# Two products of the identity with itself ahead of the low products of later weight pieces

## The chip, the cores and the metric

The kernel runs on one core of a Trainium2 chip. The time is device microseconds of one execution; the median of three runs of the kernel before is given below, and one further execution was taken with the hardware profiler. The engines are TensorE (PE, with its weight loads as PEld), VectorE (DVE), ScalarE (ACT), GpSimd (POOL) and SyncE (SP, which issues all transfers here).

## What is computed

A gated linear attention over 768 steps (4 batches of 8 heads of 48), then two feed-forward layers on its output. Cut to what matters:

```python
for t in range(S):                                   # attention, state 48x48 per head
    state = alpha[t] * state + outer(k[t], v[t])
    y[t] = q[t] @ state
h = relu(x @ w_in)                                   # first layer, 384 -> 1024
conv = sum(conv_w[k] * shifted(h, k) for k in range(3))
x = (h * sigmoid(conv)) @ w_out                      # 1024 -> 384
xn = (x - mean(x)) / sqrt(var(x) + 1e-6) * g_ln      # second layer
out = x + relu(xn @ w_ch1) @ w_ch2                   # 384 -> 1536 -> 384
```

The weights arrive as 64-bit floats.

## The kernel before

The 24 attention chunks (128 steps each, chunk 0 to 23) are computed in a parallel form: two scans on DVE give the running products of alpha (`later`, `a`), POOL multiplies them into k and q, PE makes scores `s`, DVE masks them (`pm`), PE makes the output `y` and the state update `u`. Two chunks make a block of 256 rows; there are 12 blocks. A block goes through the first layer (`h`, 8 groups of 128 columns, then `acc`), the norm, a turn on PE (`h<-ident,xn`, halves 0 and 1, each split by ACT and DVE into `xnh` and `xnl`) and the second layer (`h<-xnh`, 12 groups, then `acc`).

Every product is made from a high and a low half of its operands. The four weights are called w1 (`w_in`), w2 (`w_out`), w3 and w4; each comes in pieces of two groups (4 pieces of w1 and w2, 6 of w3 and w4). `convert_weight` makes one piece: ACT writes a scaled copy `z` (L257) and the top bits (L261), DVE joins them in two instructions (L264, L267), ACT writes the high half (L306). The low half of w1, w2 and the first half of w4 is made by PE in `low_products`: identity times `z` (L310) less the high half (L311) into a PSUM bank, which ACT copies out (L314). This is done for group i = 0 and i = 1 of the piece. There are two `z` tiles and two PSUM banks of the tag `att`, used in turn; from chunk 3 on the attention uses these banks too.

The order of the instructions on every engine is set by `Plan`: each step has an engine, an estimated time, the tiles that it reads and writes, and a turn. `order` plays the steps with these estimates and writes each engine's list down; on the chip every engine then follows its list in order, and a step that waits holds up what stands behind it. So a step that is added, or one estimate, can move steps of every engine. Tiles that are handed out with `new` are handed out in the order in which the steps were added.

Of the kernel before, what the change touches and what calls it, by code (L numbers as in the profile page):

```python
# [21 lines left out]
DM = H * D  # L22
# [33 lines left out]
CONVERT_PACE = 1.25, 1, 1   # L56
BY_PE = 2, 0
LATER = 0, 8
LOW2 = "pool" 
LOWS = "pe", "pe", "pool", "pe"   # L60


class Plan:
# [11 lines left out]
    def ring(self, tag, n):  # L75

        self.sizes[tag] = n
        m = self.made[tag] = self.made.get(tag, -1) + 1
        return (tag, m)

    def add(self, engine, us, fn, r=(), w=(), new=(), port=False, mode=None, chain=None):

        if self.direct:
            fn()
            return
        me = len(self.steps)
        w = list(w) + list(new)
        needs = {self.wrote[b] for b in list(r) + w if b in self.wrote}
        for b in w:
            needs.update(self.read.get(b, ()))  # L90
        starts = set()
        for b in new:
            key = b[0], chain
            if key in self.first:
                starts.add(self.first[key])
            self.first[key] = me
        for b in r:
            self.read.setdefault(b, set()).add(me)
        for b in w:
            self.wrote[b], self.read[b] = me, set()  # L100
        needs.discard(me)
        starts.discard(me)
        mine = [b for b in set(list(r) + w) if b[0] in self.sizes]
        for b in mine:
            self.uses[b] = self.uses.get(b, 0) + 1
        new = [b for b in new if b[0] in self.sizes]
        self.steps.append((engine, us, fn, needs, starts - needs, port, mode, self.turn, mine, new))
# [93 lines left out]
def act_us(n, scaled=False):  # L201
    return 0.165 + 0.00083 * n + 0.093 * scaled


def dve_us(n, rate=1):
    return 0.15 + 0.00104 * rate * n


def pool_us(n):
    return 0.13 + 0.00215 * n  # L210
# [7 lines left out]
def attn_moe_kernel(ctx: ExitStack, tc, qka, vv, qka_t, v_t, w_in, conv_w, w_out, g_ln, w_ch1, w_ch2, out):  # L218
    nc = tc.nc
    pe, act, dve, pool, sp = nc.tensor, nc.scalar, nc.vector, nc.gpsimd, nc.sync  # L220
    plan = Plan()
    add, ring = plan.add, plan.ring
# [4 lines left out]
    ident = const.tile([128, 128], F32, name="ident")  # L227
# [6 lines left out]
    low = const.tile([R, NC], F32, name="low")  # L234
# [13 lines left out]
    def bank(tag, name):  # L248
        return psum.tile([128, 512], F32, tag=tag, name=name, bufs={"h": HB, "acc": NT + 1, "att": 2}[tag])

    def from_f64(z, raw, n):

        low, high = raw[:, :n, 0], raw[:, :n, 1]
        zi = z.bitcast(I32)

        def first():
            act.activation(out=z, in_=high.bitcast(F32), func=ACTF.Copy, scale=2.0 ** -112)  # L257

        def top():
            byte = raw[:, :n, :].bitcast(U8)[:, :, 3]  # L260
            act.activation(out=low, in_=byte, func=ACTF.Copy, scale=1 / 32, bias=-15.5 / 32)  # L261

        def join():
            dve.scalar_tensor_tensor(  # L264
                out=zi, in0=zi, scalar=3, in1=low, op0=ALU.logical_shift_left, op1=ALU.bitwise_or
            )
            dve.scalar_tensor_tensor(  # L267
                out=zi, in0=high, scalar=-(2 ** 31), in1=zi, op0=ALU.bitwise_and, op1=ALU.bitwise_or
            )

        yield first
        yield top
        yield join
# [3 lines left out]
    def weight_tile(n, j, dtype):  # L277
        return const.tile([128, PIECE, 2, DM], dtype, tag=f"w{n}_{j}", name=f"w{n}_{j}", bufs=1)
# [12 lines left out]
    def convert_weight(n, dst, j):  # L291
        m, w, z = PIECE * DM, (f"w{n}", j), ring("z", ZB)
        t = {}

        def first():
            t["z"] = wk.tile([128, m], F32, tag="z", name="z", bufs=ZB)
            raw = raw_w.pop((n, j)).rearrange("p j s f -> p (j s f)")
            t["f"] = list(from_f64(t["z"], raw.rearrange("p (n w) -> p n w", w=2), m))
            t["f"][0]()

        def high():
            t["w"] = weight_tile(n, j, F32R)
            for i in range(PIECE):
                dst[j * PIECE + i] = t["w"][:, i]
            t["z"] = t["z"].rearrange("p (j f) -> p j f", j=PIECE)
            act.activation(out=t["w"][:, :, 0], in_=t["z"], func=ACTF.Copy)  # L306

        def low_products(i):
            t[i] = bank("att", "low")[:, :DM]
            pe.matmul(out=t[i], lhsT=ident, rhs=t["z"][:, i], start=True, stop=False)  # L310
            pe.matmul(out=t[i], lhsT=minus, rhs=t["w"][:, i, 0], start=False, stop=True)  # L311

        def low_half(i):
            act.activation(out=t["w"][:, i, 1], in_=t[i], func=ACTF.Copy)  # L314

        def rest(engine):
            engine.tensor_tensor(out=t["w"][:, :, 1], in0=t["z"], in1=t["w"][:, :, 0], op=ALU.subtract)

        add("act", act_us(m), first, r=[w], new=[z])
        add("act", act_us(m), lambda: t["f"][1](), w=[w])  # L320
        add("dve", 2 * dve_us(m), lambda: t["f"][2](), r=[w], w=[z], port=True)
        add("act", act_us(m), high, r=[z], w=[w])
        low = LOW2 if n > 2 and j >= F2 // 2 // PIECE else LOWS[n - 1]
        if low == "pe":
            for i in range(PIECE):
                b = ring("att", 2)
                add("pe", 0.9, lambda i=i: low_products(i), r=[z, w], new=[b], mode="full")
                add("act", act_us(DM), lambda i=i: low_half(i), r=[b], w=[w])
        elif low == "dve":
            add("dve", dve_us(m), lambda: rest(dve), r=[z], w=[w], port=True)  # L330
        else:
            add("pool", pool_us(m), lambda: rest(pool), r=[z], w=[w], port=True)
# [9 lines left out]
    raw, vraw, prep, post, att = {}, {}, {}, {}, {}  # L342
# [584 lines left out]
            act.activation(out=hi[:, :, t:t + n], in_=src, func=ACTF.Copy)  # L927
            dve.tensor_tensor(out=lo[:, :, t:t + n], in0=src, in1=hi[:, :, t:t + n], op=ALU.subtract)

    def warm(n):  # L930

        ps = bank("h", "warm")
        for _ in range(n):
            pe.matmul(out=ps[:, :128], lhsT=ident, rhs=ident, start=True, stop=True)

    def load_small():
        t = {}

        def load():
            sp.dma_start(out=cwr.rearrange("p n w -> p (n w)"), in_=conv_w.bitcast(I32))  # L940
            sp.dma_start(out=gl, in_=g_ln.rearrange("(o f) -> o f", o=1).to_broadcast([128, DM]))
            t["f"] = list(from_f64(cw.rearrange("p k j -> p (k j)"), cwr, 3 * F1))

        add("sp", dma_us(220), load, new=[("cwr", 0)])
        add("act", act_us(24), lambda: t["f"][0](), r=[("cwr", 0)], w=[("cw", 0)])
        add("act", act_us(24), lambda: t["f"][1](), w=[("cwr", 0)])
        add("dve", 0.36, lambda: t["f"][2](), r=[("cwr", 0)], w=[("cw", 0)])
# [4 lines left out]
    def at(turn, fn, *args):  # L952

        plan.turn = turn
        fn(*args)
# [8 lines left out]
    begin, n = {}, 0  # L964
# [5 lines left out]
    def end(s, i):  # L970
        part = len(parts_of(s, i)) - 1
        j0, j1 = parts_of(s, i)[part]
        return begin[s, i, part] + j1 - j0
# [32 lines left out]
    def weight(n, j):  # L1006
        l, c = LOADS[n], CONVERT[n]
        if n > 1 and j >= F2 // 2 // PIECE:
            l, c = l + LATER[0], c + LATER[1]
        at(l + LOAD_PACE * PIECE * j, load_weight, n + 1, sources[n], j)  # L1010
        at(c + CONVERT_PACE[min(n, 2)] * PIECE * j, convert_weight, n + 1, (w1, w2, w3, w4)[n], j)
# [28 lines left out]
    for s, i, part in up:  # L1040
# [4 lines left out]
        if s == 0:  # L1045
            w = m + F1 - 1 + LAG
            calls.append((min(w, begin[1, i, 0] - 0.2), norm, i))
            w += WAIT
            if i >= XN:
                w = max(w, end(1, i - XN) - 1)  # L1050
# [120 lines left out]
```

## Time and profile before

| | |
|---|---|
| median of 3 runs | 686.26 us (684.97, 686.26, 686.45) |
| the profiled execution | 685.02 us, its span 683.2 us |
| PE busy in the span | 649.7 us (95%) |
| DVE, ACT, POOL busy | 432.5, 328.6, 123.9 us |
| data moved | 44.5 MB, nearly all of the weights in the first 62 us |

The page gives each engine's busy time and the granted clock of TensorE in 40 slices of 17 us. A busy PE is not PE at its peak. The first four slices have gaps on PE, the rest none to speak of, so the stages of the start have to be read apart from the whole.

### The profile page before, as it was taken

The numbers are of one execution on the slowest core, as the hardware profiler recorded it, in microseconds if no ns is written. First come the engines' busy times: TensorE is split into PE (matmuls) and PEld (weight loads), VectorE is DVE, ScalarE is ACT, GpSimd is POOL, SyncE is SP. The second block draws the span as 40 slices with busy tenths as digits, with TensorE's granted clock in tenths as the row PEclk, the third lists the DMA queues.
The fourth block names the chain that finished last, engine by engine and source line by source line (L and its number), as shares of the span: only waits on it lengthen the run. The fifth ranks groups of instructions, "written<-read, shape, count | busy, mean of one in ns | idle before, by whom it ended". The sixth has DMA issues, their size and how long they took to land.

```text
span 683.2 us, 14211 instructions
## 1 busy us (share of the span) xinstructions
PE 649.7 (95%) x5788; PEld 612.6 (90%) x5788; DVE 432.5 (63%) x865; ACT 328.6 (48%) x795; POOL 123.9 (18%) x190
## 2 busy tenths in 40 slices
PE   3887999999999999999999999999999999999995
PEld 2546887989999999999999999999999999999994
DVE  5586999898468379448468379358468457365221
ACT  3678799755245236345345346345245335254210
POOL 4052342461121031101021031101021000000000
PEclk9979999999999999999999999999999999999998
DMA  9997201112112012102012012102001000000000
GB/s 316 319 393 229 71 2 48 52 57 64 57 58 76 5 57 81 57 1 80 1 58 79 2 58 80 57 1 81 1 16 39 1 2 24 1 24 1 2 24 27
DMA packets 15736, 44.50 MB, mean 65 GB/s; under 512 B 1472, under 2 KB 4672, under 8 KB 15664
## 3 DMA queue, kind: packets, MB, share of 16 engines
q1 hardware_dynamic: 15664, 43.52, 19.5%
q8 instruction: 47, 0.77, 0.5%
q14 instruction: 25, 0.20, 0.1%
HBM read 38.80 MB, written 4.72 MB: 64 GB/s over the span
## 4 chain that ended last, share of the span: by engine, by line
PE 89%; DVE 4%; ACT 3%; DMA 1%; issue 1%; POOL 0%; SPq 0%; ACTq 0%
PE acc L690 37%; PE h L803 23%; PE h L604 15%; PE y L518 5%; PE s L450 4%; PE u L534 2%; PE low L310 1%; PE h L759 1%; DMA raw<-in_qka 1%; PE kt L474 1%; DVE z L267 1%; DVE z L264 1%; ACT w L261 1%; ACT z L257 0%; ACT w L314 0%
## 5 line engine op out<-in xcount | busy, mean ns | idle before, releaser
L690 PE MATMUL acc<-w,gh 128*128 128x384 f32 x960 | 250.9, 342 | 0.0
L690 PEld LDWEIGHTS acc<-w,gh 128*128 128x128 f32 x960 | 160.9, 188 | 3.4 <-issue 0.8
L690 PE MATMUL acc<-w,gl 128*128 128x384 f32 x480 | 161.3, 336 | 0.0
L816 DVE SCALAR_TENSOR_TENSOR gl<-h,gh 128x256 fp32r<-128x256 f32 x144 | 60.4, 422 | 153.8 <-ACT gh L811 151.9
L811 ACT ACTIVATE gh<-h 128x256 fp32r<-128x256 f32 x144 | 55.3, 384 | 186.5 <-PE acc L690 168.3
L803 PE MATMUL h<-xnh,w 128*128 128x256 f32 x864 | 127.5, 283 | 0.0
L803 PEld LDWEIGHTS h<-xnh,w 128*128 128x128 f32 x864 | 118.4, 188 | 1.0 <-DVE a L424 0.4
L620 DVE SCALAR_TENSOR_TENSOR cv<-h,cw,cv 128x256 f32<-128x256 f32 x192 | 92.2, 481 | 28.5 <-ACT cv L616 24.0
L604 PE MATMUL h<-xh,w 128*128 128x258 f32 x576 | 87.4, 288 | 4.4 <-ACT gl L658 3.3
L690 PEld LDWEIGHTS acc<-w,gl 128*128 128x128 f32 x480 | 90.1, 188 | 0.0
L604 PEld LDWEIGHTS h<-xh,w 128*128 128x128 f32 x576 | 79.5, 191 | 7.7 <-ACT gl L658 4.5
L803 PE MATMUL h<-xnl,w 128*128 128x256 f32 x432 | 74.9, 282 | 0.0
L612 ACT ACTIVATE h<-h 128x258 f32<-128x258 f32 x96 | 35.7, 372 | 61.7 <-PE h L604 59.2
L803 PEld LDWEIGHTS h<-xnl,w 128*128 128x128 f32 x432 | 61.6, 188 | 0.0
L604 PE MATMUL h<-xl,w 128*128 128x258 f32 x288 | 50.4, 283 | 0.0
L635 ACT ACTIVATE cv<-cv 128x256 f32<-128x256 f32 x96 | 39.7, 415 | 21.1 <-DVE cv L620 20.8
L616 ACT ACTIVATE cv<-h,cw 128x256 f32<-128x256 f32 x96 | 45.3, 473 | 1.6
L638 DVE TENSOR_TENSOR h<-h,cv 128x256 f32<-128x256 f32 x96 | 40.6, 424 | 8.2 <-ACT cv L635 5.5
L411 POOL COPY ends<-later 112x4 f32<-112x4 f32 x24 | 5.9, 245 | 217.6 <-DVE later L408 217.6
L428 POOL TENSOR_TENSOR a<-raw,a 112x512 f32<-112x512 f32 x24 | 30.1, 1254 | 69.7 <-DVE a L424 68.4
L604 PEld LDWEIGHTS h<-xl,w 128*128 128x128 f32 x288 | 41.6, 191 | 0.2 <-POOL xl L580 0.2
L652 ACT ACTIVATE gh<-h 128x256 fp32r<-128x256 f32 x96 | 35.8, 380 | 10.2 <-DVE h L638 8.6
(90 smaller groups left out, 778.6 us busy)
## 6 DMA issues: line engine op xcount, KB each, us to landing
raw<-in_qka SPq DMA_DIRECT2D x23, 673.8 KB, 4.7
w<-in_moe_w_ch SPq DMA_DIRECT2D x12, 768.0 KB, 15.3
vraw<-in_vv SPq DMA_DIRECT2D x24, 256.0 KB, 2.7
out<-x SPq DMA_DIRECT2D x11, 384.0 KB, 2.8
w<-in_moe_w_in SPq DMA_DIRECT2D x4, 768.0 KB, 13.3
w<-in_moe_w_out SPq DMA_DIRECT2D x4, 768.0 KB, 14.4
raw<-in_qka SPq DMA_DIRECT2D x1, 448.0 KB, 3.8
out<-x SPq DMA_DIRECT2D x2, 192.0 KB, 3.8
```

The lines of the kernel that those rows point to most:

```text
L518: pe.matmul(out=ps[32 * n:32 * n + 32, k * C:(k + 1) * C], lhsT=l, rhs=r, start=m < 4, stop=m >= len(products) - 4, skip_group_check=True,)
L604: pe.matmul(out=ps[:, :T + 2], lhsT=w1[j][:, l, k * 128:(k + 1) * 128], rhs=r[:, k, :], start=n == 0, stop=n == 3 * K1 - 1,)
L612: act.activation(out=t["h"], in_=t["h"], func=ACTF.Relu)
L616: act.activation(out=t["cv"], in_=t["h"][:, 0:T], func=ACTF.Copy, scale=cw[:, 0, j:j + 1])
L620: dve.scalar_tensor_tensor(out=t["cv"], in0=t["h"][:, k:k + T], scalar=cw[:, k, j:j + 1], in1=t["cv"], op0=ALU.mult, op1=ALU.add,)
L635: act.activation(out=t["cv"], in_=t["cv"], func=ACTF.Sigmoid)
L638: dve.tensor_tensor(out=t["h"][:, :T], in0=t["h"][:, 1:T + 1], in1=t["cv"], op=ALU.mult)
L652: act.activation(out=m_t[0, i, j][0], in_=t["h"][:, :T], func=ACTF.Copy)
L690: pe.matmul(out=acc_t[s, i][t][:, :DM], lhsT=l[:, ts], rhs=w[j][:, r], start=j in firsts and n == 0, stop=j + 1 in lasts and n == 2,)
L803: pe.matmul(out=ps[:, :T], lhsT=w3[j][:, l, k * 128:(k + 1) * 128], rhs=r[:, k, :], start=n == 0, stop=n == 3 * K1 - 1,)
L811: act.activation(out=m_t[1, i, j][0], in_=u["ps"][:, :T], func=ACTF.Relu)
L816: dve.scalar_tensor_tensor(out=lo, in0=u["ps"][:, :T], scalar=0.0, in1=hi, op0=ALU.max, op1=ALU.subtract)
```

## The change

`convert_weight` gets a function `fill`. It takes the PSUM bank that `low_products` of group 0 used to take, and writes two products of the identity with itself (128 by 128) into it; `low_products` then starts the bank anew, so nothing of them is left in a result. It is added ahead of the low products of group 0 for pieces 1 to 3 of w1 and of w2, that is six times, with an estimate of 0.44 us for each. A function `warm` that nothing called goes.

```diff
+FILL = 2
...
+        def fill():
+
+            t[0] = bank("att", "low")[:, :DM]
+            for _ in range(FILL):
+                pe.matmul(out=t[0][:, :128], lhsT=ident, rhs=ident, start=True, stop=True)
+
         def low_products(i):
-            t[i] = bank("att", "low")[:, :DM]
+            if i not in t:
+                t[i] = bank("att", "low")[:, :DM]
...
                 b = ring("att", 2)
-                add("pe", 0.9, lambda i=i: low_products(i), r=[z, w], new=[b], mode="full")
+                filled = i == 0 and n < 3 and j > 0
+                if filled:
+                    add("pe", 0.22 * FILL, fill, new=[b], mode="full")
+                add("pe", 0.9, lambda i=i: low_products(i), r=[z, w], mode="full", **{"w" if filled else "new": [b]})
```

The planned order of all engines changes between the second piece of the weights and the second block. Three places of it follow. In the names, `w1_2` is piece 2 of w1, and the last number is the buffer's. Lines below L308 are one to eleven higher after the change.

**Place 1, the third chunk and piece 2.** DVE before, from the first scan of chunk 2 (`later_331`) to its first mask (`pm_401`):

```order
L408 SCALAR_TENSOR_TENSOR later_331<-raw_185,from_one_78 112x516
L264 SCALAR_TENSOR_TENSOR z_326<-z_326,w1_2_122 128x768
L267 SCALAR_TENSOR_TENSOR z_326<-w1_2_122,z_326 128x768
L414 RECIPROCAL from_end_79<-later_331 112x4
L264 SCALAR_TENSOR_TENSOR cw_64<-cw_64,cwr_66 128x24
L267 SCALAR_TENSOR_TENSOR cw_64<-cwr_66,cw_64 128x24
L424 SCALAR_TENSOR_TENSOR a_359<-raw_185,from_end_79 112x516
L408 SCALAR_TENSOR_TENSOR later_371<-raw_275,from_one_78 112x516
L264 SCALAR_TENSOR_TENSOR z_361<-z_361,w2_2_127 128x768
L267 SCALAR_TENSOR_TENSOR z_361<-w2_2_127,z_361 128x768
L459 TENSOR_TENSOR pm_401<-s_384,mask_63 128x512
```

DVE after, the same stretch:

```order
L419 SCALAR_TENSOR_TENSOR later_333<-raw_185,from_one_78 112x516
L265 SCALAR_TENSOR_TENSOR cw_64<-cw_64,cwr_66 128x24
L268 SCALAR_TENSOR_TENSOR cw_64<-cwr_66,cw_64 128x24
L425 RECIPROCAL from_end_79<-later_333 112x4
L435 SCALAR_TENSOR_TENSOR a_349<-raw_185,from_end_79 112x516
L265 SCALAR_TENSOR_TENSOR z_335<-z_335,w1_2_122 128x768
L268 SCALAR_TENSOR_TENSOR z_335<-w1_2_122,z_335 128x768
L419 SCALAR_TENSOR_TENSOR later_374<-raw_275,from_one_78 112x516
L265 SCALAR_TENSOR_TENSOR z_364<-z_364,w2_2_127 128x768
L268 SCALAR_TENSOR_TENSOR z_364<-w2_2_127,z_364 128x768
L470 TENSOR_TENSOR pm_403<-s_379,mask_63 128x512
```

The second scan of chunk 2 (`a`) stood behind the two joins of w1's piece 2 and now stands ahead of them, and the two masks `pm` have no join between them any more.

PE before, from the low products of w2's piece 1 to the first score of chunk 2:

```order
L310 MATMUL low_337<-z_310,ident_61 128x384
L311 MATMUL low_337<-w2_1_333,minus_62 128x384
L310 MATMUL low_345<-z_310,ident_61 128x384
L311 MATMUL low_345<-w2_1_333,minus_62 128x384
L310 MATMUL low_355<-z_326,ident_61 128x384
L311 MATMUL low_355<-w1_2_350,minus_62 128x384
L310 MATMUL low_368<-z_326,ident_61 128x384
L311 MATMUL low_368<-w1_2_350,minus_62 128x384
L450 MATMUL s_384<-a_359,later_331 128x128
```

PE after, the same stretch with two of the six fills:

```order
L313 MATMUL low_329<-ident_61 128x128 x2
L318 MATMUL low_329<-z_312,ident_61 128x384
L319 MATMUL low_329<-w2_1_337,minus_62 128x384
L318 MATMUL low_354<-z_312,ident_61 128x384
L319 MATMUL low_354<-w2_1_337,minus_62 128x384
L313 MATMUL low_358<-ident_61 128x128 x2
L318 MATMUL low_358<-z_335,ident_61 128x384
L319 MATMUL low_358<-w1_2_370,minus_62 128x384
L461 MATMUL s_379<-a_349,later_333 128x128
```

The fills stand directly behind the low products of the piece before, and the scores of chunk 2 now stand ahead of the second group of w1's piece 2 (`low_399`, which comes behind them).

**Place 2, the first product of the first layer.** PE before, from the low products of w1's piece 3:

```order
L310 MATMUL low_471<-z_374,ident_61 128x384
L311 MATMUL low_471<-w1_3_414,minus_62 128x384
L310 MATMUL low_484<-z_374,ident_61 128x384
L311 MATMUL low_484<-w1_3_414,minus_62 128x384
L604 MATMUL h_495<-xh_198,w1_0_206 128x258 x6
L604 MATMUL h_495<-xl_203,w1_0_206 128x258 x3
L604 MATMUL h_508<-xh_198,w1_0_206 128x258 x6
```

PE after, from the second group of w2's piece 2:

```order
L318 MATMUL low_469<-z_364,ident_61 128x384
L319 MATMUL low_469<-w2_2_405,minus_62 128x384
L313 MATMUL low_475<-ident_61 128x128 x2
L615 MATMUL h_494<-xh_198,w1_0_206 128x258 x6
L615 MATMUL h_494<-xl_203,w1_0_206 128x258 x3
L318 MATMUL low_475<-z_418,ident_61 128x384
L319 MATMUL low_475<-w1_3_485,minus_62 128x384
L615 MATMUL h_514<-xh_198,w1_0_206 128x258 x6
L615 MATMUL h_514<-xl_203,w1_0_206 128x258 x3
L318 MATMUL low_525<-z_418,ident_61 128x384
```

Two pairs of low products of w1's piece 3 that stood ahead of the first `h` now stand between the first three `h`, with a fill ahead of the first pair. On DVE the joins of that piece stood between the two masks of chunk 2 and now stand behind both, and behind the second scan of chunk 3; chunk 2's `xl` stands behind them in both orders, and the addition to the state now behind `xl`.

**Place 3, the turned half 1 of block 0.** ACT before, from the second low half of w4's piece 2 to the second `xnh`:

```order
L314 ACTIVATE w4_2_1167<-low_1196 128x384
L658 ACTIVATE gl_1207<-h_1103 128x256
L635 ACTIVATE cv_1199<-cv_1199 128x256
L306 ACTIVATE w3_3_1222<-z_1122 128x2x384
L652 ACTIVATE gh_1231<-h_1143 128x256
L257 ACTIVATE z_1240<-w4_3_343 128x768
L769 ACTIVATE xnh_1201<-h_1225 128x3x128
```

ACT after, from the high half of w3's piece 3 to the second `xnh`:

```order
L307 ACTIVATE w3_3_1232<-z_1160 128x2x384
L663 ACTIVATE gh_1236<-h_1107 128x256
L663 ACTIVATE gh_1239<-h_1147 128x256
L262 ACTIVATE w4_3_351<-w4_3_351 128x768
L669 ACTIVATE gl_1274<-h_1107 128x256
L669 ACTIVATE gl_1278<-h_1147 128x256
L258 ACTIVATE z_1280<-w3_4_532 128x768
L408 ACTIVATE raw_725,low_68<-raw_725 112x4x128
L576 ACTIVATE xh_853<-y_1245 128x3x128
L780 ACTIVATE xnh_1190<-h_1282 128x3x128
```

Counted from the program's start, ACT has five instructions more ahead of the second `xnh` than before, and none less: the top of w4's piece 3, a `gl`, the `z` of w3's piece 4, a check of `raw` (L408) and the `xh` of chunk 5. On PE the first product of the second layer has the same products ahead of it in both orders, but for the fills.

## Rows read from the trace of the kernel before

**Rows 1.** Stages: length, busy PE, PEld, DVE, ACT, POOL, granted clock, DMA, GB/s.

```profile
28.00:62.00 34.00, 24.40 (x160) 14.91 (x158) 25.16 (x33) 26.81 (x48) 11.50 (x12) 0.85 1.04 349
62.00:90.00 28.00, 27.06 (x299) 24.48 (x299) 24.38 (x43) 22.25 (x54) 10.73 (x13) 0.94 0.20 61
90.00:119.30 29.30, 26.40 (x213) 23.16 (x212) 27.45 (x46) 28.41 (x65) 9.45 (x11) 1.00 0.09 25
...
150.00:674.00 524.00, 524.00 (x4689) 508.00 (x4689) 310.87 (x683) 218.87 (x571) 66.82 (x115) 1.00 0.12 36
```

**Rows 2.** PE's timeline, 34 to 62 us: start, us, instruction, [idle before <-releaser].

```profile
34.16 0.88 PE L310 MATMUL low<-z,ident 128*128 128x384 f32 x2 [3.05 <-ACT w L261]
...
42.30 1.16 PE L450 MATMUL s<-a,later 48*128 48x128 f32 x16 [0.62 <-POOL a L428]
...
45.22 1.27 PE L310 MATMUL low<-z,ident 128*128 128x384 f32 x2 [1.23 <-DVE z L267]
...
48.34 1.15 PE L518 MATMUL y<-a,state 112*32 112x128 f32 x24
...
53.86 0.99 PE L604 MATMUL h<-xh,w 128*128 128x258 f32 x6 [1.06 <-POOL xh L580]
...
57.47 0.81 PE L310 MATMUL low<-z,ident 128*128 128x384 f32 x2
57.82 0.63 PE L311 MATMUL low<-w,minus 128*128 128x384 f32 x1
...
61.80 0.39 PE L354 MATMUL h<-gh,minus 128*128 128x256 f32 x1 [2.52 <-ACT gh L652]
```

**Rows 3.** Half-microseconds of PE: length, busy PE, granted clock, DMA share, GB/s.

```profile
35.00:35.50 0.50, 0.50 (x3) 0.84 0.99 371
...
42.00:42.50 0.50, 0.20 (x2) 0.84 1.03 399
...
45.50:46.00 0.50, 0.50 (x2) 0.58 1.04 406
```

**Rows 4.** Timeline of PE, the first product of the second layer.

```profile
119.29 0.88 PE L803 MATMUL h<-xnh,w 128*128 128x256 f32 x6
```

**Rows 5.** Timeline of ACT, 116 to 121 us, from the second `xnh`.

```profile
116.11 0.48 ACT L769 ACTIVATE xnh<-h 128x384 fp32r<-128x384 f32 x1
116.58 0.38 ACT L658 ACTIVATE gl<-h 128x256 fp32r<-128x256 f32 x1
116.86 0.95 ACT L261 ACTIVATE w<-w 128x768 int32<-128x768 uint8 x1
117.70 0.92 ACT L257 ACTIVATE z<-w 128x768 f32<-128x768 f32 x1
118.52 0.47 ACT L565 ACTIVATE xh<-y 128x384 fp32r<-128x384 f32 x1
...
120.06 0.62 ACT L397 ACTIVATE raw<-raw 112x512 f32<-112x512 f32 x1
```

**Rows 6.** Timeline of DVE, the second `xnl` of block 0.

```profile
118.08 0.53 DVE L778 TENSOR_TENSOR xnl<-h,xnh 128x384 fp32r<-128x384 f32 x1
```

**Rows 7.** Timeline of DVE, 35 to 52 us.

```profile
35.07 0.93 DVE L264 SCALAR_TENSOR_TENSOR z<-z,w 128x768 int32<-128x768 int32 x1
36.04 1.96 DVE L267 SCALAR_TENSOR_TENSOR z<-w,z 128x768 int32<-128x768 int32 x1
...
38.86 1.28 DVE L424 TENSOR_TENSOR_SCAN a<-raw,from_end 112x516 f32<-112x516 f32 x1
...
43.09 1.98 DVE L267 SCALAR_TENSOR_TENSOR z<-w,z 128x768 int32<-128x768 int32 x1
...
51.09 0.72 DVE L545 TENSOR_TENSOR state<-u,state 48x192 f32<-48x192 f32 x2 [1.42 <-PE u L534]
51.85 0.56 DVE L571 TENSOR_TENSOR xl<-y,xh 128x384 fp32r<-128x384 f32 x1
```

**Rows 8.** Timeline of ACT, the load of the sigmoid's table.

```profile
59.00 1.28 ACT L635 ACT_TABLE_LOAD   x1
```

More of the change, by code (lines that the diff above doesn't have):

```diff
@@ L928, in general_x @@
             dve.tensor_tensor(out=lo[:, :, t:t + n], in0=src, in1=hi[:, :, t:t + n], op=ALU.subtract)
[L930 to L934, printed above, removed]
     def load_small():
```

## The prediction

> **What bounds the kernel now.** I read the stages first [rows 1]. From 150 to 674 us PE is busy 524.00 of 524.00 us at a granted clock of 1.00: nothing but PE's own work sets that part, and the change leaves its work alone there. So the time is decided by when PE comes into this state. In 28 to 62 us PE is idle for 34.00 - 24.40 = 9.60 us, in 62 to 90 for 0.94, in 90 to 119.3 for 2.90: 13.4 us that can be won or added to. The same rows show who holds PE up. In 28 to 62 us the transfers run at full share (1.04), DVE and ACT have idle time (8.8 and 7.2 us), and PE waits in turn for conversions of weights and for chunk 2. In 90 to 119.3 us ACT is busy 28.41 of 29.30 us: there ACT sets the pace.
>
> Then PE's timeline [rows 2]. It waits 3.05 us at 34.16, 1.23 us at 45.22, 1.06 us for the first product `h` of the first layer at 53.86, and 2.52 us at 61.80 for ACT. The clock [rows 3] falls to the lower of its two levels (1.2 GHz) at about 35.3 us, comes back to 2.4 GHz at 42.2 and falls again at 45.6.
>
> The marker that I use for everything is the first product of the second layer, at 119.29 us [rows 4]; ahead of it PE has the same products in both orders but for the six fills, and from there it hardly waits. It needs the second `xnh` of ACT (116.11, next instruction 116.58) [rows 5] and the second `xnl` of DVE (118.08, 0.53 us) [rows 6]. At present neither is late: `xnl` ends 0.68 us before PE comes.
>
> **The change part by part.** *The fills.* No row shows the identity against itself. The nearest is the identity against 384 columns of `z`: the next product starts 0.35 us behind it [rows 2]. Two products of 128 columns cost a third each if columns set the price, 2 x 0.12 = 0.23 us, and 2 x 0.35 = 0.70 us if something fixed does; twice that at the lower clock. I take 0.4 us, since 128 columns are nearer to a third. Six would be 1.4 to 4.2 us, but five stand where PE waits: directly behind the products of the piece before, ahead of products that wait for a join or, for the fifth, ahead of the first `h`, which waits for POOL. Their cover is those waits (3.05, 1.23, 1.06 us among them). The sixth stands between the first `h` products, where PE has work: 0.4 us on the path (0.2 to 0.7). If all covers went it would be the whole 4.2. Could a fill gain by itself? Only through the clock; that is a rival below.
>
> *DVE's order, place 1.* The second scan of chunk 2 moves ahead of the two joins of w1's piece 2. These ran from 35.07 to 38.00 = 2.93 us, the scan from 38.86 [rows 7]. So the scan starts at 38.86 - 2.93 = 35.93 and ends at 37.21 (1.28 us), and the joins end 2.93 later, at 40.14 instead of 38.00. What follows on DVE, up to the end of the joins of w2's piece 2 at 43.09 + 1.98 = 45.07, has the same instructions ahead of it and stays. The scores of chunk 2 (before at 42.30) [rows 2] need the scan and POOL, and stand behind one pair of low products of w1's piece 2; with the join at 40.14 and ACT's high half (some 0.8 us, an estimate from the 0.92 us of the same-sized `z` in rows 5) they come at about 41.3. Both masks then follow 45.07 directly.
>
> *The first `h`, place 2.* From 45.07 to `xl` of chunk 2 at 51.85, DVE did two masks, two joins, a scan, then waited 1.42 us for PE's update `u`, and added it to the state from 51.09 [rows 7]. Now the masks come without a join between them, so `y` and `u` are done before DVE needs them, and the addition stands behind `xl`: 1.42 + (51.85 - 51.09) = 2.18 us less. `xl` comes at 49.7 and the first `h` at 53.86 - 2.2 = 51.7. Two pairs of low products that stood ahead of it, about 1.0 us each (57.47 to 57.82 + 0.63) [rows 2], now come between the `h` products; this is PE's work moved, not lost, since PE waits again until 61.80 for ACT, which loads the sigmoid's table at 59.00 [rows 8]. With `h` 2.2 us earlier that load can be 2.2 us earlier too.
>
> *ACT's order, place 3.* Five more instructions stand ahead of the second `xnh`. By [rows 5] a top of a piece is 0.95 us, a `z` 0.92, a `gl` 0.38, an `xh` 0.47, a check 0.62: 3.34 us, less 0.1 each by which such instructions overlap (the `gl` at 116.58 lasts 0.38, the next starts at 116.86), so 2.9 us. If ACT works without a gap, the second `xnh` is over at 116.58 + 2.9 = 119.5 less G, where G is the idle time that ACT loses ahead of it; `xnl` adds 0.6, so the marker comes at 120.1 - G instead of 119.29. The gain is G - 0.8, and 0.4 less for the sixth fill.
>
> *G.* ACT's idle time is 7.2 us in 28 to 62, 5.75 in 62 to 90 and 0.9 in 90 to 119.3 [rows 1]. The 2.2 us by which the first `h` comes earlier go straight out of the first. Of the second I take a quarter, 1.4 us, since part of it is ACT waiting for products that PE now makes earlier; nothing and half (2.9) are its bounds. G = 3.6, between 2.2 and 5.1.
>
> **The sum:** 3.6 - 0.8 - 0.4 = 2.4 us faster. Against the profiled execution, 685.02 us (its span of 683.2 and 1.8 around it), that is 682.6. This execution lies at the low end of the three runs, whose mean is 685.9; against that it is 683.5, which I give.
>
> **The rivals.** *The fills hold the clock.* What the rows show: the clock fell right behind a wait of 3.05 us, but at 45.5 also behind one of 1.23 us [rows 2, 3]. A fill stands at the near end of its wait and shortens 3.05 to 2.3 us at best, so I expect the falls to stay. If it held, the low products of 45.22 and what follows up to `y` at 48.34, 3.1 us at half speed, would give back 1.6 us; the 0.94 of 62 to 90 us stands for 2 x 0.06 x 28 = 3.4 us at half speed with PE busy, 1.7 more. With 2.4 that is 4.0 faster, 681.9, and 680.2 with both. The Trainium skill, "TensorE: Matmul & The Clock Gate", section "Why this matters for your kernels", asks to leave no long idle gaps between bursts of matmuls, or the clock drops. By that rule alone the fills would help at the longest wait and would not be needed at the 1.23 us one; the trace shows a fall there too, so it bears the rule out only in part.
>
> *ACT takes it back.* The first `h` is earlier, but ACT keeps its idle time of the second stage, because the waits there are chains through PE and DVE: G = 2.2, gain 1.0, time 684.9. For it speaks that ACT is at 97% in 90 to 119.3 us; against it that PE already has its work then.
>
> *The `z` tile comes free too late; slower.* The second group of w1's piece 2 now stands behind the scores and the turn of chunk 2. Only when it is done is there a `z` for w1's piece 3, whose joins stand ahead of `xl` on DVE, and so of the first `h`. Scores at 41.3, 1.16 us [rows 2], the turn about half of that, a pair 1.0: done at 44.1, or 46.8 if the clock is at its lower level all along; then a copy, a `z` and a top on ACT, some 2.4 us: 46.5 to 49.2. DVE wants them at 49.7 less two joins of 0.93 = 47.8. So at the higher clock there are 1.3 us to spare, at the lower 1.4 are lost. From a start after 50.2 on, with nothing won in the second stage, this ends over 1.4 us slower; at 51.4 it would be 3.6 - 2.2 + 0.8 + 0.4 = 2.6 slower, 688.5.
>
> *The change moves nothing.* The planned lists show that it does, so this gets no chance of its own.
>
> **How the numbers follow.** 0.2%, 1.4 us, is about what a measurement of this kernel can tell from no change. My forecast (G 3 to 5) 0.48; the clock held 0.12; ACT takes it back, or part of the lateness of `z` eats the gain, 0.24; clearly slower 0.16. Faster 0.60, within 0.2% 0.24, slower 0.16. The range leaves out half of the slower case and half of the clock's: 681.0 to 687.2. The forecast's own is 682.0 to 684.5.
>
> **What would show it.** First `h` at 51 to 52 us (a start after 53.9 speaks for the `z` rival); the clock still at its lower level for some 7 us between 35 and 46, in contrast to the first rival; ACT's idle time in 62 to 90 us under 5; the first product of the second layer at 116.5 to 117.5, with a short wait for `xnl`; PE without a gap for the 524 us that follow its first 30 us [rows 1]. I am wrong if PE loses time behind the marker, or if the fills cost more than 0.7 us each.

## The result

After the change the median is 691.02 us (686.93 to 695.19, 14 runs), beside 686.20 us for the kernel before (682.52 to 686.88, 14 runs). The recorded ratio, which is of the runs and not of the two medians (those give 1.0070), is 1.0084, with a 95% interval of 1.0063 to 1.0105: slower, where I forecast 683.5 us with a range up to 687.2. The profiled execution took 692.51 us (span 690.7, mean granted clock 0.977); before it was 685.02 (683.2, 0.985).

### The profile page after: what moved, and what is told of

Its sections match the earlier page's. It is cut to its first block, busy times and chain, and to the rows that moved or that the text cites. A ratio compares the mean times of both kernels' runs of the same rounds, so it can differ in the third digit from the quotient of the medians.

```text
span 690.7 us, 14267 instructions
## 1 busy us (share of the span) xinstructions
PE 657.5 (95%) x5812; PEld 621.6 (90%) x5812; DVE 433.4 (63%) x865; ACT 328.4 (48%) x795; POOL 124.5 (18%) x190
## 4 chain that ended last, share of the span: by engine, by line
PE 89%; DVE 4%; ACT 3%; DMA 1%; issue 1%; POOL 0%; SPq 0%; ACTq 0%; DVEq 0%
PE acc L701 36%; PE h L814 22%; PE h L615 15%; PE y L529 6%; PE s L461 4%; PE low L318 2%; PE u L545 2%; DVE z L268 1%; PE kt L485 1%; PE h L770 1%; DMA raw<-in_qka 1%; DVE z L265 1%; ACT z L258 1%; ACT w L307 1%; ACT w L262 1%
## 5 line engine op out<-in xcount | busy, mean ns | idle before, releaser
L701 PEld LDWEIGHTS acc<-w,gh 128*128 128x128 f32 x960 | 162.6, 190 | 3.6 <-issue 0.6
L822 ACT ACTIVATE gh<-h 128x256 fp32r<-128x256 f32 x144 | 55.3, 384 | 188.2 <-PE acc L701 169.7
L615 PE MATMUL h<-xh,w 128*128 128x258 f32 x576 | 88.9, 291 | 3.9 <-ACT gl L669 3.9
L461 PE MATMUL s<-a,later 48*128 48x128 f32 x384 | 31.9, 304 | 11.3 <-POOL later L431 9.1
```

Source lines behind the costliest of these rows:

```text
L461: pe.matmul(out=t["ps"][g][:, p * C:(p + 1) * C], lhsT=kt[r, p, :], rhs=qd[r, NP - 1 - p, :], start=True, stop=True,)
L615: pe.matmul(out=ps[:, :T + 2], lhsT=w1[j][:, l, k * 128:(k + 1) * 128], rhs=r[:, k, :], start=n == 0, stop=n == 3 * K1 - 1,)
L701: pe.matmul(out=acc_t[s, i][t][:, :DM], lhsT=l[:, ts], rhs=w[j][:, r], start=j in firsts and n == 0, stop=j + 1 in lasts and n == 2,)
L822: act.activation(out=m_t[1, i, j][0], in_=u["ps"][:, :T], func=ACTF.Relu)
```

## The profile after

The stages of the changed kernel, to be held against [rows 1]: length, busy PE, PEld, DVE, ACT, POOL, granted clock, DMA share, GB/s.

```profile
28.00:62.00 34.00, 27.73 (x185) 19.78 (x185) 25.41 (x36) 25.57 (x49) 11.21 (x12) 0.83 1.03 355
62.00:90.00 28.00, 27.29 (x304) 24.82 (x304) 22.60 (x39) 21.94 (x52) 8.67 (x10) 0.96 0.22 62
90.00:119.30 29.30, 23.39 (x131) 20.39 (x129) 24.99 (x42) 24.40 (x57) 9.91 (x11) 0.88 0.04 9
119.30:150.00 30.70, 29.26 (x239) 27.79 (x240) 25.73 (x35) 19.80 (x39) 14.79 (x13) 0.89 0.24 70
150.00:674.00 524.00, 524.00 (x4733) 507.69 (x4732) 316.15 (x692) 222.80 (x578) 71.70 (x120) 1.00 0.12 36
```

The first stage came out as the change meant it: PE is idle 6.3 us there instead of 9.6. The third and fourth are new: PE loses 3 us more to waits in 90 to 119.3, and its clock, 1.00 before in both, is 0.88 and 0.89. Of the kernel before, the fourth stage is not among the rows above:

```profile
119.30:150.00 30.70, 30.01 (x263) 28.92 (x263) 27.92 (x43) 19.95 (x40) 17.20 (x14) 1.00 0.17 49
```

PE's timeline of the changed kernel up to 62 us, the counterpart of [rows 2] (start, us, instruction, [idle before <-releaser]):

```profile
28.00 0.64 PE L313 MATMUL low<-ident 128*128 128x128 f32 x4
28.47 0.81 PE L318 MATMUL low<-z,ident 128*128 128x384 f32 x2
...
40.74 2.08 PE L461 MATMUL s<-a,later 48*128 48x128 f32 x16
...
50.78 0.60 PE L313 MATMUL low<-ident 128*128 128x128 f32 x4
51.14 0.97 PE L615 MATMUL h<-xh,w 128*128 128x258 f32 x6
...
60.06 0.39 PE L365 MATMUL h<-gh,minus 128*128 128x256 f32 x1 [2.30 <-ACT gh L663]
```

A fill of two products takes 0.36 us at the higher clock (50.78 to 51.14), 0.18 us each. The first `h` comes at 51.14 instead of 53.86. And then the marker, in place of [rows 4]:

```profile
127.11 0.88 PE L814 MATMUL h<-xnh,w 128*128 128x256 f32 x6
```

It is 7.82 us later, and the whole span is 7.5 us longer: from the marker to the end it is 563.6 us, before 563.9. Everything that the change costs lies between 51 and 127 us. Here is the place, first before the change, PE from 93 to 100 us:

```profile
93.60 0.99 PE L604 MATMUL h<-xh,w 128*128 128x258 f32 x6 [0.47 <-ACT gl L658]
...
94.79 0.81 PE L310 MATMUL low<-z,ident 128*128 128x384 f32 x2
...
96.64 0.99 PE L604 MATMUL h<-xh,w 128*128 128x258 f32 x6 [0.74 <-ACT gl L658]
...
97.94 0.81 PE L310 MATMUL low<-z,ident 128*128 128x384 f32 x2
...
98.76 0.88 PE L604 MATMUL h<-xh,w 128*128 128x258 f32 x6
```

and after it, 92 to 120 us:

```profile
92.44 0.99 PE L615 MATMUL h<-xh,w 128*128 128x258 f32 x6 [0.47 <-ACT gl L669]
...
94.13 0.39 PE L365 MATMUL h<-gh,minus 128*128 128x256 f32 x1 [0.34 <-ACT gh L663]
95.49 1.66 PE L615 MATMUL h<-xh,w 128*128 128x258 f32 x6 [0.97 <-ACT gl L669]
...
98.48 1.66 PE L615 MATMUL h<-xh,w 128*128 128x258 f32 x6 [0.47 <-ACT gl L669]
...
102.25 0.81 PE L318 MATMUL low<-z,ident 128*128 128x384 f32 x2
...
115.92 0.46 PE L461 MATMUL s<-a,later 48*128 48x128 f32 x2 [0.57 <-ACT w L322]
117.86 1.16 PE L461 MATMUL s<-a,later 48*128 48x128 f32 x14 [1.48 <-ACT w L322]
119.66 0.86 PE L365 MATMUL h<-gh,minus 128*128 128x256 f32 x2 [0.65 <-ACT gh L663]
120.45 1.51 PE L529 MATMUL y<-a,state 112*32 112x128 f32 x24
```

Before, the two low pairs of w4's second piece (94.79, 97.94) stood between the `h` groups of block 1 and filled PE's time there. In the new list that piece is converted later and its pairs stand behind these groups (the first at 102.25). Four short waits follow one another, 2.25 us in 92.0 to 98.5, and behind the third of them the six `h` products take 1.66 us instead of 0.99. The same again from 115 us on, where the scores of chunk 5 wait for two banks just taken by the low pairs of w4's third piece. The clock in stretches of two microseconds (columns as in the stages):

```profile
94.00:96.00 2.00, 0.90 (x3) 0.70 (x4) 2.00 (x3) 2.00 (x7) 1.18 (x1) 0.78 0.00 0
96.00:98.00 2.00, 2.00 (x10) 1.71 (x8) 1.93 (x4) 0.88 (x2) 0.00 (x0) 0.50 0.00 0
...
102.00:104.00 2.00, 2.00 (x12) 1.73 (x11) 1.33 (x3) 0.73 (x3) 0.95 (x2) 1.00 0.00 0
118.00:120.00 2.00, 1.35 (x15) 1.16 (x16) 2.00 (x5) 2.00 (x5) 0.59 (x1) 0.75 0.78 231
120.00:122.00 2.00, 2.00 (x34) 1.67 (x37) 1.40 (x2) 1.96 (x4) 1.24 (x1) 0.50 0.40 114
```

The clock goes to 1.2 GHz in the third wait of each row (the 0.78 of 94 to 96 puts it at about 95.1 us, the 0.75 of 118 to 120 at about 119.0) and stays there while PE works without a gap (96 to 98, 120 to 122). No single wait in front of these falls was over 1.5 us, and single ones of 1.30 us (at 109.8) and, before the change, of 1.16 us (at 107.6) were not followed by a fall. The Trainium skill, "TensorE: Matmul & The Clock Gate", section "A second HAM failure mode: psum-queue depth-cycling", tells of a kernel whose PE idles briefly but often between groups of matmuls and whose clock goes to and fro; the rows here agree.

**An account of PE's time.** From such rows, taken in half-microseconds, I add up two losses: the idle time (length less busy PE), and what busy time at the lower level costs (busy PE times one less the granted clock). In us, from one profiled execution each:

| kernel | idle 28:62 | 62:90 | 90:119.5 | 119.5:150 | low clock 28:62 | 62:90 | 90:119.5 | 119.5:150 |
|---|---|---|---|---|---|---|---|---|
| before | 9.6 | 0.9 | 2.9 | 0.7 | 4.3 | 1.7 | 0 | 0 |
| after | 6.3 | 0.7 | 6.1 | 1.2 | 5.6 | 1.2 | 3.0 | 3.1 |

Idle: 3.5 saved up to 90 us, 3.7 lost behind it. Low clock: 0.8 more up to 90, 6.1 more behind it. The twelve identity products add 12 x 0.18 = 2.2. The sum is 9.2; measured are 7.5. The account closes to about 2 us, also in the runs below when they are held against the kernel before (one needs the time outside 28 to 150 us for it), and is not read finer than that. The difference of two runs' accounts can be off by more.

## The experiments

The kernel before ran beside each: 685.28 us (22 runs) with the first four, 684.63 (23) with the next four, 685.20 (19) with the last four. Ratios are the recorded ones of the runs to these, not quotients of the medians.

**Order and fills apart.** The list of the changed kernel without the identity products:

```diff
         def fill():
             t[0] = bank("att", "low")[:, :DM]
-            for _ in range(FILL):
-                pe.matmul(out=t[0][:, :128], lhsT=ident, rhs=ident, start=True, stop=True)
```

> The changed kernel's planned order on every engine, with the six fills planned and their bank taken but none of their 12 products issued. My theory now (the late planned order is what costs: between 90 and 127 us the new lists leave holes on PE in which the clock falls): as slow as the change, 689 to 692 us, with the first product of the second layer at 125 us or later. Rival (the fills' own time and waits on PE cost): back to before, 685 to 687 us.

Measured: 691.25 us, 1.0073 [1.0048, 1.0098]; the marker stands at 126.57. The third stage:

```profile
90.00:119.30 29.30, 23.05 (x127) 20.06 (x126) 25.54 (x43) 24.42 (x57) 9.78 (x12) 0.87 0.05 14
```

So the list makes the loss without the products. The other half, the list of before with the products in it:

```diff
             t[i] = bank("att", "low")[:, :DM]
+            for _ in range(2 if i == 0 and n < 3 and j > 0 else 0):
+                pe.matmul(out=t[i][:, :128], lhsT=ident, rhs=ident, start=True, stop=True)
```

> The order of before on every engine, with the two identity products issued ahead of the same six low products, unknown to the planner. Theory of the late order: like before within 1.4 us, 685 to 687.5 us, first product of the second layer at 119 to 120 us. Rival of the fills' own cost: 689 to 691 us.

Measured: 682.41 us, 0.9961 [0.9948, 0.9974]: faster than both kernels, which neither theory had (685 to 687.5 or 689 to 691). The first two stages:

```profile
28.00:62.00 34.00, 26.30 (x194) 18.02 (x192) 25.18 (x33) 26.66 (x50) 11.50 (x12) 0.90 1.03 349
62.00:90.00 28.00, 27.06 (x305) 24.64 (x302) 25.62 (x46) 23.27 (x56) 11.96 (x14) 1.00 0.22 63
```

Against [rows 1] the clock is 0.90 for 0.85 and 1.00 for 0.94. It is back at the higher level at 36.1 us instead of 42.2, and the fall after 62 us is gone. The account: 1.9 us less idle time, 3.0 less at the low clock, 2.2 for the products; 2.7 in all, and the span is 2.6 shorter.

**Early and late part of the list.** Two lists are planned in one kernel, and a run uses one of them up to the last first-layer `h` of block 0 and the other one behind it.

```diff
...
-        plan.emit()
+        a, b = ([p.steps[n][2] for n in p.order()] for p in (plan, other))
+        hs = [m for m, f in enumerate(a) if f.__qualname__.endswith("moe1_a.<locals>.products")]
+        first = a[:hs[F1 - 1] + 1]
+        done = set(map(id, first))
+        for fn in first + [f for f in b if id(f) not in done and f.__name__ != "fill"]:
+            fn()
...
```

> The changed kernel's planned lists (fills issued) up to the last product of the first layer of block 0, then everything that is left in the order of the kernel before. Theory of the late order: the 2 to 3 us that the first product of the first layer comes earlier are kept or lost to ACT, 683 to 686.5 us, never over 688. Rival (the early order, chunk 2 first, is what costs later): 689 to 692 us.

Measured: 685.20 us, 0.999 [0.9976, 1.0004].

> The order of before up to the last product of the first layer of block 0, then everything that is left in the changed kernel's order; no fills. Theory of the late order: slow, 689 to 693 us, holes on PE between 92 and 127 us and the lower clock in them. Rivals (fills, or the early order): 685 to 687 us.

Measured: 693.34 us, 1.0097 [1.0064, 1.0131]. The third stage, first of the new early part with the old late one, then the reverse:

```profile
90.00:119.30 29.30, 26.36 (x212) 23.11 (x211) 27.63 (x46) 28.41 (x65) 9.44 (x11) 1.00 0.09 25
```

```profile
90.00:119.30 29.30, 24.80 (x131) 21.63 (x129) 25.72 (x41) 24.37 (x58) 11.18 (x11) 0.88 0.00 1
```

The late part carries the loss whatever stands in front of it. The early part, fills included, is worth nothing that can be told from the kernel before, although its first `h` starts at 50.36 us: it saves 3.3 us of idle time up to 62, and then 1.3 go to waits in 62 to 90, 0.8 to the clock and the rest to the products themselves.

**Is it the clock or the waits?** With identity products behind each take of the high part from an `h` of block 1, in unused columns of that bank, here four:

```diff
...
             less(t["h"][:, :T], m_t[0, i, j][0])
+            for _ in range(4 if i == 1 else 0):
+                pe.matmul(out=t["ps"][:, 384:512], lhsT=ident, rhs=ident, start=True, stop=True, skip_group_check=True)
```

> The order of the changed kernel, with 44 products of the identity with itself added where PE waits late: four behind each product that takes the high part off a group's h in block 1's first layer (in columns of that bank that nothing reads), eight behind the second low product of w4's last piece (likewise). Theory 1: between 92 and 127 us the short waits let the granted clock fall, and the lower level, some 14 us of 92 to 128 us, is what costs the changed kernel its time. Then the clock of 90:119.3 goes from 0.88 to 0.97 or more and of 119.3:150 from 0.89 to 0.97, the first product of the second layer comes at 121 to 123 us instead of 127.1, and the time is 684 to 687. Theory 2: the waits of that order (on ACT's copies, and on the two banks of the last low pairs) make the time by themselves, the clock only goes along. Then the clock rises, but the first product of the second layer stays behind 125.5 and the time is 689 to 692.

The eight products behind the low product that this text speaks of did not get in: the edit named w3's third piece, whose low half GpSimd makes. 32 were added. Measured: 692.33 us, 1.0111 [1.0084, 1.0138]. PE and ACT in it:

```profile
91.20 0.28 PE L368 MATMUL h<-gh,minus 128*128 128x256 f32 x1
91.32 1.05 PE L679 MATMUL h<-ident 128*128 128x128 f32 x8
92.84 1.00 PE L618 MATMUL h<-xh,w 128*128 128x258 f32 x6 [0.47 <-ACT gl L672]
```

```profile
92.41 0.38 ACT L672 ACTIVATE gl<-h 128x256 fp32r<-128x256 f32 x1 [1.03 <-PE h L679]
```

The clock is 1.00 from 90 to 150 us and the `h` products take 1.00 us again, but ACT's copy waits for the products (1.03 us), since they write the bank that it reads, and PE's next group waits for the copy. What the clock gave back, 6.1 us, went for the most part into 32 x 0.18 = 5.8 us of products. PE's idle time of 90 to 150 us fell too, from 7.3 to 4.9 us, so that by the account some 2.7 us should be left; the span is 0.4 us shorter. As it stood, the run could not tell the theories apart, so I repeated it with one product each, eight in all (`range(1 ...)` in the same lines):

> The order of the changed kernel, with one product of the identity with itself (in columns of that bank that nothing reads) behind each of the eight products that take the high part off block 1's h: 8 more products, where the run before had 32. There the clock of 90 to 150 us came back to 1.00, but the 32 products took some 7.8 us of TensorE themselves, and ACT's copy of the low part waited for them. Theory 1: the low clock is worth some 6 us of the loss and one product per wait keeps it up in part at a quarter of the price (about 2 us): the products of 90 to 150 us that run at the lower level lose 0 to 3 us instead of 6.1, and the time is 686 to 689. Theory 2: the clock only goes along with waits that ACT sets: the clock may rise, the waits grow by as much, time 690.5 to 692.5.

Measured: 688.24 us, 1.0045 [1.0022, 1.0067]; the marker stands at 120.86.

```profile
90.00:119.30 29.30, 23.72 (x199) 20.64 (x198) 27.21 (x43) 26.56 (x60) 10.07 (x9) 1.00 0.09 25
119.30:150.00 30.70, 29.63 (x223) 28.90 (x223) 25.94 (x40) 19.87 (x40) 16.35 (x16) 1.00 0.20 54
```

Nothing else of the list has changed, eight more products are in it, and its median is 2.8 us under that of the changed kernel (1.0045 to 1.0084; the intervals overlap by 0.0004). The profiled execution is 5.3 us shorter; about 2.7 of that come from its first two stages, where the clock was 0.90 and 1.00 this time and PE idle 1.2 us longer (low clock 2.9 us instead of 6.8). The eight products, all behind 89 us, can't have made that. So some 2.6 us of this execution come from behind 90 us, where the account has 5.3 (6.1 for the clock, 0.6 of idle time, less 8 x 0.18 = 1.4 for the products). PE's idle time of 90 to 150 us stays (6.7 us, 7.3 in the changed kernel), and so does 0.45% of loss.

One execution can't settle the price of the clock, but the mean clocks of all runs are on record, and they price it without an added product. In the changed kernel the five runs at 0.974 to 0.977 took 692.5 to 695.2 us, the eight at 0.980 to 0.983 took 688.4 to 692.0, and the one at 0.986, the clock of the kernel before, 686.93. The two other runs of its late list at 0.984 and 0.986, one without the products and one behind the old early part, took 686.73 and 687.29. So at the clock of before the list is 0.7 to 2.0 us slower than the kernel before, and some 4 of the changed kernel's 5 to 6 us go with the clock. The held runs fit: at 0.985 to 0.987 the six with 32 products lie 4.2 to 6.2 us above 686.93 (5.8 of products) and the four with eight 1.3 to 2.8 us (1.4 of products); the batches of the kernel before differ by up to 1.6 us, so this is rough. By themselves the runs show only that time and clock go together; with the eight products, which change the clock by an edit, the low clock is a cause of the loss and not only a companion of the waits. Where in an execution the clock was low is seen only in the profiled ones.

**The banks of chunk 5's scores.** The low half of w4's third piece on GpSimd, in the list of the changed kernel:

```diff
...
+                def products(i=i):
+                    if (n, j) not in ((4, 2),):
+                        low_products(i)
+                    elif i == 0:
+                        rest(pool)
...
```

(ACT's two copies of that piece fall away.)

> The order of the changed kernel, word for word but for w4's last early piece: its low half is made by one subtraction on GpSimd (1.84 us in this trace) instead of the two low pairs on TensorE (0.8 us each) and ACT's two copies. So the score products of chunk 5 find their two banks free. Theory 1 (the waits of 0.57 and 1.48 us for those banks and the low clock behind them carry a part of the loss): the first product of the second layer comes at 122 to 125 us instead of 127.1, time 686 to 689. Theory 2 (the scores wait anyway, for GpSimd's product, which in the changed kernel ends at 115.4 and here is held up by the subtraction): the wait stays 1.5 us or longer, only the 1.6 us of the pairs are saved or not even these, time 689 to 692.

Measured: 689.92 us, 1.0087 [1.0064, 1.0111].

```profile
116.47 0.85 PE L376 MATMUL h<-gh,minus 128*128 128x256 f32 x2 [5.10 <-ACT gh L674]
```

The marker comes at 123.31, and the span of the profiled execution is 2.6 us shorter, but the ratio is that of the changed kernel: the marker came where the first theory had it, the time where the second had it. The waits for the banks are gone, and one for ACT's `gh` of 5.10 us stands in their place: PE has nothing else ahead of that product in its list, and ACT's list has a `z`, a top and a high half of weights ahead of that `gh`. With both edits:

> Both of the two edits before: one identity product behind each of the eight takes, and the last early piece's low half on GpSimd. If clock and bank waits are two separate parts of the loss, the gains add up: the sum of the two runs' gains within 1.5 us, at best 683 to 686. If they are one and the same (whatever keeps PE busy there gives it back), the gain is no more than the larger of the two.

Measured: 690.31 us, 1.0088 [1.0066, 1.011]. The two do not add up, and the gain of the first is gone too; a wait of 4.89 us for `gh` is left, in which none of the eight products stands, and the clock is 0.92 in 90:119.3.

**The planner's number.** The same products, with another estimate for a fill:

```diff
-                    add("pe", 0.22 * FILL, fill, new=[b], mode="full")
+                    add("pe", 0.0, fill, new=[b], mode="full")
```

> The changed kernel with one number other: the planner is told that a pair of identity products takes 0.00 us instead of 0.44; the products are the same. The list comes out otherwise: the two low pairs of w4's piece 1 stand between the h products of block 1 again, as before the change. Theory 1: the time goes by where the list puts those low pairs (PE's late holes and the clock in them): 681 to 685, clock 0.97 or more in 90:119.3. Theory 2: any list planned with the fill steps loses, because they take the bank of the low pair earlier and shift the conversions: 688 to 692.

Measured: 691.74 us, 1.0101 [1.007, 1.0132].

> The changed kernel with the fill steps planned at 0.22 us instead of 0.44. Here too the low pairs of w4's piece 1 stand between the h products, but the two low pairs of w4's last piece stand with a group's products between them. Theory 1 (the place of the low pairs in the late part decides): 681 to 685 and a clock of 0.97 or more in 90:119.3. Theory 2 (every list planned with the fills loses): 688 to 692.

Measured: 683.23 us, 0.9987 [0.9966, 1.0008]. The third stage of the one and of the other:

```profile
90.00:119.30 29.30, 24.81 (x151) 20.69 (x151) 25.66 (x45) 26.91 (x64) 10.15 (x12) 1.00 0.00 1
```

```profile
90.00:119.30 29.30, 25.30 (x194) 21.52 (x195) 25.54 (x43) 26.31 (x62) 9.33 (x10) 0.94 0.09 25
```

Both expectations miss half. With 0.22 us the list is as good as before, so not every list with fills loses. With nothing it loses as much as the changed kernel, though w4's low pairs are back between the `h` groups and the clock is 1.00: so the place of these pairs does not decide alone. By the account this run has 1.1 us more idle time than before in 28 to 150 us and 1.6 us more at the low clock; with the products that is 4.9 of the 9.1 us by which its span is longer. Another 1.5 are idle time ahead of 28 us (PE busy 15.70 us there, before 17.16) and 0.8 idle time and low clock behind 150, which leaves 1.9. Its waits grew by 5.4 us in 62 to 150 us. Why that list makes them is open.

**How many products.** Six per fill instead of two, then one, in the list of before (both texts say five later pieces; there are six, three of each weight):

> The list of the kernel before with six identity products instead of two ahead of the first low product of each of the five later pieces of w1 and w2. With two, the time was 682.4 and the clock of 28:62 0.90, with a low stretch left at 42.9 to 46.2 us. Theory 1 (fills in the waits keep the clock up, and more of them more so): the low stretch shrinks, the clock of 28:62 is 0.93 or more, time 680.5 to 682.5. Theory 2 (four more products of about 0.11 to 0.25 us each outgrow the waits and delay the low pair behind them): five fills delay by 0.3 to 0.6 us each, first h at 53.5 or later, time 683.5 to 686.

Measured: 685.99 us, 1.002 [1.0003, 1.0037]. The clock of 28:62 is 0.95, which the first theory wanted; PE's busy time there is 27.87 us for 24.40. Against the kernel before the account has 3.5 us less idle time and 2.6 less at the low clock, and the 36 products cost 36 x 0.18 = 6.5 us: they take what they give. The clock of 62:90 is 0.94, as before the change; with two products it was 1.00.

> The list of the kernel before with one identity product instead of two ahead of the first low product of each of the five later pieces of w1 and w2. Two gave 0.9961 of the time before, six 1.002. If two products' gain is the clock's early rise at 36 us and the missing low stretch at 62 to 66 us, one product gives half of it or nothing: 0.997 to 1.0 (683 to 685.3). If the products' own time is what limits the gain (0.2 us each, on the path), one gives more than two: 0.994 to 0.996.

Measured: 685.22 us, 0.9989 [0.9967, 1.0011]. The twelve runs lie in two groups: eight at a granted clock of 0.986, 684.9 to 686.9 us, and four at 0.990, 680.3 to 681.4. With two products nine of eleven runs have 0.990 or 0.991, and one more 0.995. The kernel before has the faster group too, without any product, but rarely: of its 64 runs beside these, two are at 0.990 and 0.991, with 680.7 and 680.0 us. So the products do not give a fixed gain; they make the executions with the higher clock more frequent.

## Why the prediction was wrong

**Right.** The first `h`: forecast 51.7, measured 51.14. DVE's order, place 1: forecast 35.93 for the scan and 40.14 for the end of the joins; measured 34.75 and 37.46 + 1.83 = 39.29. `xl` of chunk 2: 49.7, measured 49.92, in part by luck, since the masks came earlier than I had them (44.30 for 45.07) and a wait that I had not came behind them (below). A fill: 0.4 us taken, 0.36 measured at the higher clock. That most of them stand where PE waits: its idle time of 28 to 62 us fell by 3.3 us, of which the products themselves fill up to 2.2. PE without a gap from 150 us on.

**The step that failed is G**, ACT's idle time ahead of the second `xnh`, above all its third term: I took 2.2 us less idle time in 28 to 62 us and 1.4 less in 62 to 90, 3.6 us of gain, and put the change in 90 to 119.3 at nothing. These are ACT's and DVE's rows of the changed kernel in place of [rows 5, 6]:

```profile
124.53 0.49 ACT L780 ACTIVATE xnh<-h 128x384 fp32r<-128x384 f32 x1 [0.31 <-PE h L770]
```

```profile
125.06 0.56 DVE L789 TENSOR_TENSOR xnl<-h,xnh 128x384 fp32r<-128x384 f32 x1 [0.87 <-ACT xnh L780]
```

ACT's next instruction starts at 124.92 instead of 116.58, 8.3 us later. From 28 us to there ACT is busy 76.26 us, before 74.76, and idle 20.66 us, before 13.82. So the added work came to 1.5 us where I took 2.9, and G to 13.82 - 20.66 = -6.8 us, not +3.6. By the stages, ACT's idle time was 7.2 + 5.8 + 0.9 us and is 8.4 + 6.1 + 4.9, with 1.3 more up to the second `xnh`: the earlier first `h` took nothing off the first two terms (the sign that I had named, under 5 us in the second, failed), and the third grew by 4.0. I had read 28.41 of 29.30 us in [rows 1] as "there ACT sets the pace", and so let ACT work through whatever order it was given. It is not so in the new list: ACT waits for PE (1.17 us for an `h` product ahead of 98.04, 1.65 for a low pair ahead of 103.27), which runs at half its clock from about 95 to 102 us, and PE for ACT. The sum has no term for a lower clock behind 90 us either; by their mean clocks the runs price the lower clock at some 4 us.

Two things were in my reach. I looked at place 3 for how many instructions stand ahead of `xnh`, and not at what stood between PE's waits of 0.47 and 0.74 us at 93.60 and 96.64: two low pairs that the new list takes away. And I used [rows 3] only for the first stage. They showed that the clock falls behind a wait of 1.23 us; I noted it, and did not ask where else such waits would arise.

**The rivals.** "The fills hold the clock" was half right: with the list of before they do so (0.90 for 0.85, 682.4 us), but 681.9 is near that by luck: it holds 2.4 us of gain from the new list, which that run does not have. The clock's own terms, 1.6 + 1.7 = 3.3 us, were near (3.0 by the account). With the list of the change the fills do not hold it (0.83). "ACT takes it back" had the right engine, but as an idle time that stays, not as one that grows. Of the slower side I had only the `z` tile. The wait that it foresaw did come on DVE, ahead of the joins of w1's piece 3:

```profile
47.98 0.96 DVE L265 SCALAR_TENSOR_TENSOR z<-z,w 128x768 int32<-128x768 int32 x1 [1.12 <-ACT w L262]
```

It made PE wait nowhere up to the first `h` at 51.14, since PE had other products until then. The chance of 0.16 was too small because I priced a new list by the three places of it that I had read.

## What to carry to other kernels

A step added to a planned list is two changes, its own work and a new list; make them apart (the same list with the work, the new list without it) before either is judged. In a new list look for what stood in the short waits of the engine that sets the time, and on TensorE count what its clock loses behind a row of such waits: here some 4 to 6 us, where the waits themselves had grown by 3.7 us. A busy share of 97% in a stage doesn't show that an engine will set the pace in another order.

## What the hardware showed that I had not expected

The granted clock fell to 1.2 GHz in a row of waits of 0.34 to 0.97 us (92 to 95.5 us). With eight identity products of 0.18 us each, one behind each take of block 1, it stayed at 2.4 GHz from 90 to 150 us in the profiled execution (0.88 to 1.00), and the mean clock of all eight runs was 0.985 to 0.992, against 0.974 to 0.983 in 13 of the changed kernel's 14. Runs of one kernel differ by it: the changed kernel's go from 686.9 us at a mean clock of 0.986 to 695.2 at 0.974, while the 22 runs of the kernel before in the first batch lie at 0.985 to 0.987 and 683.5 to 686.9 us.
